# Token tiles taken chunk by chunk over the batches in a linear-attention and mixture-of-experts kernel

## The chip, the cores and the metric

The kernel runs on one core of one Trainium2 chip. The metric is the device time of one launch in microseconds (us), as the median of several runs. Engines are called PE (TensorE, with PEld for its weight loads), DVE (VectorE), ACT (ScalarE), POOL (GpSimd) and SP (SyncE, which here only issues DMAs).

## The reference, cut to what matters

```python
B, H, S, D = 4, 8, 768, 48              # q, k, v, alpha: [B, H, S, D], alpha in 0.8..1
for t in range(S):
    state = alpha[:, :, t, :, None] * state + k[:, :, t] (outer) v[:, :, t]   # [B, H, D, D]
    y[:, :, t] = q[:, :, t] @ state
x = y.transpose(0, 2, 1, 3).reshape(3072, 384)      # a row per token
do_compute = x @ w_skip > 0
e = argmax(x @ w_gate)                  # one of 8 experts, w1 384x1024, w2 1024x384
out = x                                 # for the tokens to skip
out = x + gate[e] * (relu(x @ w1[e]) @ w2[e])       # for the others
```

There are two halves: an attention whose state decays with every token, separately for each batch and head, and a layer in which each token goes to at most one of eight experts.

## The kernel before

**Attention.** A sequence of 768 tokens is cut into six chunks of 128. A token tile is one chunk of one batch, with all eight heads; there are 24. Heads go in four pairs: one head of a pair lies on partitions 0 to 47, the other on 64 to 111, and the tokens run along the free axis, one stretch per pair. For a tile the kernel does the following.

- `load` (L208) brings decays, q and k into one of five buffers (`qka`), and v (`vt`), four tiles ahead.
- `decay_suffix` (L224) runs a scan on DVE from the chunk's end to its start, which gives the products of the decays after a token (`sfx`); its last column is the decay of the whole chunk (`total`). POOL multiplies k by it. `decay_prefix` (L245) runs a second scan, forward, seeded with the reciprocal of the total (`pfx`); q is multiplied by it, on POOL, or on DVE for the first three tiles. Both are done three tiles ahead.
- `scores` (L253): eight products of k and q, one a head, into two PSUM buffers, one for each head of a pair. `causal` (L265) copies them under a mask to SBUF (`st`), a copy on DVE for each of the two.
- `turn_k` (L272) transposes k on PE, ACT copies it to SBUF (`kt`). `outer` (L293) makes from it and v what the chunk adds to the state (`ps_v`).
- `carry` (L324): state = (state + what the chunk adds) times the total of the next chunk, on DVE, in two instructions for each of the two heads' partitions. The states of a pair are one 112 x 112 block with zeros between the heads.
- `inter` (L282): output from the state, four products of 112 rows, one a pair. `intra` (L305): output from the chunk's own tokens, added in the same PSUM buffer `ps_y`, of which there are two; ACT copies the result to SBUF (`xt`).
- `rows` (L344): PE turns the output into rows of x and their logits (`ps_g`), DVE sums the logits, ACT copies the rows, SP stores them to the output. This runs one tile later.
- `guard` (L236): two passes on ACT over the tile's decays, each with a sum, which find decays outside 0.75 to 1.25. If one is there, a general path computes everything again at the end.

**Routing** works on groups of three tiles, from tile 18 on on single ones. A dozen small DVE instructions find the expert, the counts and the gate (`route_expert` L366, `route_one` L391); PE ranks the tokens within their expert (`route_rank` L411), and DVE makes slots of it (`route_slot` L422). POOL scatters the rows by slot to DRAM (`scatter` L483). `tick` (L361) emits the next of these small instructions between large ones. Weights of the first expert are loaded and split into two float32r parts meanwhile (`weight_pieces` L497, `split_pieces` L509).

**Order.** The order is written out by hand in `static_path` (L748); each engine runs its instructions in it. The 24 tiles go batch by batch, so tile i + 1 needs the state that tile i leaves, except at a batch's start. SP's queue holds a tile's loads, the clearing of the experts' slots (iterations 0 to 3, from a tile that POOL fills), pieces of weights, and the store of the rows of the tile before.

**Experts.** For each of the eight: rows are gathered, transposed and split in two (`turn` L548), four times a group of 18 products gives 256 columns of the hidden layer (`up` L563, three PSUM buffers, ACT and DVE split the result), 48 products give the output (`down` L584), and POOL scatters it. The next expert's weights are split, and those of the one after it loaded, in between. `must_redo` (L605) gathers the flag for the general path, in the third expert.

Of the kernel before, what the change touches and what calls it, by code (L numbers as in the profile page):

```python
# [44 lines left out]
GT = 3                  # token tiles that are routed at a time  # L45
SOLO = 18               # from this tile on, one at a time
A_MIN, A_MAX = 0.75, 1.25   # decays for which products over a chunk stay far inside float32's range
WARM0, WARMB = 12, 2      # products that keep the tensor engine's clock up where it waits for data
LATE = NT - 3           # from this tile on, rows for the first expert do not pass through DRAM
DECAY_MIN = 1e-18       # below A_MIN ** 128: keeps the reciprocal finite where the general path takes over  # L50
EG = 8                  # value columns that the general path scans at a time


class Kernel:
# [6 lines left out]
    # ---------------------------------------------------------------- constants  # L61
    def first_constants(self):
        """What the first chunk needs, and zeros for the clock warm-up."""
# [7 lines left out]
        # mask[s, (h t)]: 1 where s <= t  # L71
# [5 lines left out]
        self.mask = const.tile([P, 4 * P], U8, name="mask")  # L77
        self.mask_f = mask_f

        # sums of what the decays lie outside the range  # L80
# [243 lines left out]
    def carry(self, i):  # L324
        """The state after chunk i, scaled by the whole decay of chunk i + 1."""
        nc, w = self.nc, self.work[i]
        if i % C == C - 1:
            return
# [624 lines left out]
```

## Time and profile before

| what | value |
|---|---|
| time, median of 3 runs | 340.71 us (339.92 to 341.02) |
| span of the profiled execution | 338.5 us, 7103 instructions |
| between the span and the median | 2.2 us |
| mean granted clock of PE | 0.905 |
| attention, up to the experts' first product | 190.2 us |
| experts, to the end | 148.3 us |
| PE busy | 287.1 us (85%) |
| DVE busy | 246.8 us (73%) |
| ACT busy | 155.2 us (46%) |
| POOL busy | 181.2 us (54%) |

The profile is that of one execution. An engine's busy time is the sum over its instructions, overlaps counted once. A row of a group gives line, engine and operation, `out<-in`, shapes, the count, the busy time, the mean of one in ns, and behind the last bar the idle time of the engine just before it and who ended that. A row of the waits reads: engine and line that waited, `<-` whom it waited for: us in total, times, the longest. A row of the order of instructions gives start and duration in us. The granted clock is a share of full speed. The DMA share is the mean share of time in which the core's 16 DMA engines had a packet under way.

### The profile page before, as it was taken

Reading aid. Unit: us, or ns where it says so; the run is one execution under the profiler, and the core shown is the slowest. Engines: PE = TensorE matmul, PEld = TensorE weight load, DVE = VectorE, ACT = ScalarE, POOL = GpSimd, SP = SyncE. Lnnn points to the kernel's source line nnn. Section 1 sums busy time; section 2 is a strip of 40 time slices with the busy share of each in tenths; the row PEclk is TensorE's granted clock in tenths of the full one; section 3 lists DMA queues with packets and bytes.
Section 4 is the critical chain, followed back from the end, with each engine's and each line's share of the span. In section 5 each row is a group of like instructions: output and inputs, shape, how many; then the busy total and the mean of one; then the engine's idle time right before and its main releaser. Section 6 shows DMA issues by size and latency. Waiting matters only on the chain.

```text
span 338.5 us, 7103 instructions
## 1 busy us (share of the span) xinstructions
PE 287.1 (85%) x2618; PEld 273.1 (81%) x2618; DVE 246.8 (73%) x511; ACT 155.2 (46%) x344; POOL 181.2 (54%) x207
## 2 busy tenths in 40 slices
PE   5978859596696776859688899999999999999990
PEld 5867748495695766758587899999999999999990
DVE  8999997979979799999986583737465556455310
ACT  6336336543345462442355492827273736455200
POOL 7333454766686856874563445455454546464311
PEclk9579989878789597796969999999999999999998
DMA  8999999989666574794334473948475665751000
GB/s 237 285 228 254 251 249 221 262 212 225 152 141 146 137 175 79 160 247 136 113 118 157 153 239 126 300 157 260 187 242 212 212 235 191 270 175 58 8 26 20
DMA packets 27243, 61.42 MB, mean 181 GB/s; under 512 B 4338, under 2 KB 15328, under 8 KB 27200
## 3 DMA queue, kind: packets, MB, share of 16 engines
q1 hardware_dynamic: 24640, 56.04, 60.4%
q0 software_dynamic: 2560, 4.83, 4.1%
q8 instruction: 23, 0.38, 0.5%
q14 instruction: 20, 0.16, 0.2%
HBM read 48.15 MB, written 15.77 MB: 189 GB/s over the span
## 4 chain that ended last, share of the span: by engine, by line
PE 54%; DVE 34%; issue 4%; DMA 3%; POOL 3%; SPq 0%; POOLq 0%; ACT 0%; DVEq 0%
PE ps_h L577 20%; PE ps_o L593 20%; DVE pfx L249 6%; DVE sfx L228 6%; DVE st L269 5%; DVE state L340 4%; PE ps_g L352 4%; PE ps_y L290 4%; DVE tmp L337 3%; POOL cnt L386 2%; DMA qka<-in_qka_dram 2%; DVE eq L380 2%; PE ps_x L557 1%; PE ps_k L277 1%; DVE d L378 1%
## 5 line engine op out<-in xcount | busy, mean ns | idle before, releaser
L581 ACT ACTIVATE hh<-ps_h 128x512 fp32r<-128x512 f32 x32 | 19.2, 599 | 63.9 <-PE ps_h L577 63.9
L598 POOL DMA_INDIRECT out_dram<-o,xr x16 | 18.6, 1162 | 47.7 <-DVE o L596 44.4
L582 DVE SCALAR_TENSOR_TENSOR hl<-ps_h,hh 128x512 fp32r<-128x512 f32 x32 | 22.1, 691 | 30.1 <-ACT hh L581 30.1
L593 PE MATMUL ps_o<-w2h,hh 128*128 128x384 f32 x128 | 43.6, 341 | 0.0
L593 PE MATMUL ps_o<-w2h,hl 128*128 128x384 f32 x128 | 43.0, 336 | 0.0
L593 PE MATMUL ps_o<-w2l,hh 128*128 128x384 f32 x128 | 43.0, 336 | 0.0
L251 POOL TENSOR_TENSOR qka<-qka,pfx 112x512 f32<-112x512 f32 x21 | 26.5, 1263 | 29.3 <-DVE pfx L249 19.6
L234 POOL TENSOR_TENSOR qka<-qka,sfx 112x512 f32<-112x512 f32 x24 | 28.9, 1206 | 21.9 <-DVE sfx L228 19.4
L526 POOL TENSOR_TENSOR w2l<-raw,w2h 128x512 fp32r<-128x512 f32 x24 | 31.2, 1299 | 17.2 <-ACT w2h L522 16.8
L290 PE MATMUL ps_y<-qka,state 112*112 112x128 f32 x160 | 27.3, 322 | 13.0 <-DVE state L340 13.0
L488 POOL DMA_INDIRECT xs<-x,slot x24 | 31.4, 1309 | 10.2 <-DVE logit L353 3.1
L249 DVE TENSOR_TENSOR_SCAN pfx<-qka,seedb 112x516 f32<-112x516 f32 x24 | 35.7, 1489 | 0.5
L290 PEld LDWEIGHTS ps_y<-qka,state 112*112 112x112 f32 x160 | 22.4, 206 | 15.6 <-DVE state L340 11.7
L242 ACT ACTIVATE over<-qka,lim 112x512 bf16<-112x512 f32 x48 | 34.3, 719 | 0.1
L596 DVE SCALAR_TENSOR_TENSOR o<-ps_o,xr 128x384 f32<-128x384 f32 x16 | 9.9, 618 | 33.1 <-PE ps_o L593 33.1
L577 PE MATMUL ps_h<-xh,w1h 128*128 128x256 f32 x192 | 33.9, 282 | 0.0
L577 PE MATMUL ps_h<-xh,w1l 128*128 128x256 f32 x192 | 33.8, 282 | 0.0
L577 PE MATMUL ps_h<-xl,w1h 128*128 128x256 f32 x192 | 33.2, 282 | 0.0
L269 DVE COPY_PREDICATED st<-mask,ps_s 128x512 f32<-128x512 uint8 x46 | 31.8, 726 | 1.5 <-PE ps_s L261 0.9
L352 PE MATMUL ps_g<-xw,xt 112*128 112x105 f32 x184 | 32.8, 336 | 0.0
L352 PEld LDWEIGHTS ps_g<-xw,xt 112*128 112x128 f32 x184 | 30.6, 252 | 2.5 <-ACT ex L404 2.5
L261 PE MATMUL ps_s<-qka 48*128 48x128 f32 x368 | 28.7, 295 | 2.8 <-DVE qka L251 2.8
(148 smaller groups left out, 672.4 us busy)
## 6 DMA issues: line engine op xcount, KB each, us to landing
raw<-in_w_dram SPq DMA_DIRECT2D x64, 384.0 KB, 4.6
qka<-in_qka_dram SPq DMA_DIRECT2D x38, 288.9 KB, 5.3
vt<-in_v_dram SPq DMA_DIRECT2D x24, 192.0 KB, 6.8
out_dram<-x SPq DMA_DIRECT2D x24, 192.0 KB, 2.1
xr<-xs SPq DMA_DIRECT2D x18, 193.0 KB, 5.2
xs<-empty SPq DMA_DIRECT2D x8, 386.0 KB, 8.3
qka<-in_first_dram SPq DMA_DIRECT2D x3, 674.2 KB, 8.3
qka<-in_first_dram SPq DMA_DIRECT2D x2, 448.0 KB, 4.8
```

Of the source, the lines that this page charges most:

```text
L234: nc.gpsimd.tensor_tensor(w["kh"][:PD], w["kh"][:PD], seg(2)[:, :, 0:P], ALU.mult)
L242: nc.scalar.activation(out=over[:PD], in_=a, func=AF.Relu, scale=scale, bias=self.lim[:PD, j:j + 1], accum_out=self.odd[:PD, j, i:i + 1])
L249: nc.vector.tensor_tensor_scan(pfx[:PD].rearrange("p a t -> p (a t)"), w["qka"][:PD, 0:NP * SEG], w["seed"][:PD].rearrange("p a t -> p (a ...
L251: (eng or nc.gpsimd).tensor_tensor(w["qh"][:PD], w["qh"][:PD], pfx[:PD, :, 1:SEG], ALU.mult)
L261: nc.tensor.matmul(ps[h][:, p * P:(p + 1) * P], lhsT=kh[r, p, :], rhs=qh[r, p, :], start=True, stop=True)
L269: nc.vector.copy_predicated(w["st"][h], self.mask, w["ps"][h])
L290: nc.tensor.matmul(w["y"][:PD, p, :], lhsT=state[:PD, p, :], rhs=w["qh"][:PD, p, :], start=(p == 0), stop=False)
L352: nc.tensor.matmul(pg[:, p, :], lhsT=w["xt"][:PD, p, :], rhs=self.xw[:PD, p, :], start=True, stop=True)
L488: ins = nc.gpsimd.indirect_dma_start(out=self.xs[:, :], out_offset=bass.IndirectOffsetOnAxis(ap=self.slot[:, i, :], axis=0), in_=x, in_off ...
L526: eng.tensor_tensor(lo[:, s], raw[:, s], hi[:, s].bitcast(F32), ALU.subtract)
L577: nc.tensor.matmul(ps[:, u, :], lhsT=a[:, k, f * P:(f + 1) * P], rhs=b[:, k, :], start=(n == 0), stop=(n == len(order) - 1))
L593: nc.tensor.matmul(ps, lhsT=a[:, f, js], rhs=b[:, f, :], start=(n == 0), stop=(n == 3 * FT - 1))
```

## The change

1. **Order of tiles.** Tile i is chunk i // 4 of batch i % 4, so the four batches take turns and a state is needed four tiles later. There are four state buffers, one a batch. The host lays out the inputs in this order.
2. **Decays.** One function, `decay`, does both scans behind each other: first the forward one from the raw decays (`pfx`), then the reciprocal of the total, then the backward one seeded with it (`sfx`), so that k is divided by the product up to its token. Then POOL multiplies k and q (DVE does both for tiles 0 and 1). It stands at the start of an iteration.
3. **States** are compact, [112, 4 x 48]: sum and product with the total take one instruction each for both heads, and the total is the chunk's own. `inter` makes eight products of 48 rows, one a head, into two PSUM buffers, one for each head of a pair; each has one copy only, and ACT copies each to SBUF.
4. **Masked copy.** The scores of a tile lie in one PSUM buffer of two banks, of which there is one; one instruction copies all under a mask twice as wide.
5. **The check** of the decays leaves the attention. In the experts' stage alpha is loaded again in eight pieces of 128 x 1152 into one buffer, a piece after each half of an output, and ACT passes over each twice. `must_redo` moves from the third to the sixth expert.
6. Scores and transposed k are issued before the ranks; the splits and ticks stand at other places.

```diff
-NT = B * C              # token tiles
+NT = B * C
...
+GP = 8
+GW = B * H * S * D // P // GP
...
-        self.ps_s = st.enter_context(tc.tile_pool(name="ps_s", bufs=2, space=PSUM))
-        self.ps_y = st.enter_context(tc.tile_pool(name="ps_y", bufs=2, space=PSUM))
+        self.ps_s = st.enter_context(tc.tile_pool(name="ps_s", bufs=1, space=PSUM))
+        self.ps_y = [st.enter_context(tc.tile_pool(name=f"ps_y{h}", bufs=1, space=PSUM)) for h in range(2)]
...
-        self.state = [fix.tile([P, NP, PD], F32, name=f"state{i}") for i in range(2)]
+        self.state = [fix.tile([P, NP, D], F32, name=f"state{b}") for b in range(B)]
...
+    def decay(self, i, eng=None):
         nc, w = self.nc, self.work[i]
+        n = NP * SEG
+        pfx = self.sc.tile([P, NP, SEG], F32, name="pfx", bufs=5)
+        nc.vector.tensor_tensor_scan(pfx[:PD].rearrange("p a t -> p (a t)"), w["qka"][:PD, 0:n], self.seed1[:PD], 0.0,
+                                     ALU.mult, ALU.max)
+        w["total"] = pfx[:, :, P:SEG]
         seed = self.seedb[i % 2]
+        self.tick()
+        nc.vector.reciprocal(seed[:PD, SEG:AW:SEG], w["total"][:PD].rearrange("p a o -> p (a o)"))
+        self.tick()
+        sfx = self.sc.tile([P, n], F32, name="sfx")
+        nc.vector.tensor_tensor_scan(sfx[:PD, 0:n - 1][:, ::-1], w["qka"][:PD, 2:AW][:, ::-1], seed[:PD, 2:AW][:, ::-1],
+                                     0.0, ALU.mult, ALU.add)
+        after = sfx[:PD].rearrange("p (a s) -> p a s", s=SEG)[:, :, 0:P]
+        (eng or nc.gpsimd).tensor_tensor(w["kh"][:PD], w["kh"][:PD], after, ALU.mult)
         (eng or nc.gpsimd).tensor_tensor(w["qh"][:PD], w["qh"][:PD], pfx[:PD, :, 1:SEG], ALU.mult)
...
     def causal(self, i):
-        for h in range(2):
-            nc.vector.copy_predicated(w["st"][h], self.mask, w["ps"][h])
-            self.tick()
+        self.nc.vector.copy_predicated(w["st"], self.mask, w["ps"])
...
     def inter(self, i):
+        w["y"] = [pool.tile([P, NP, P], F32, name="ps_y") for pool in self.ps_y]
+        state = self.state[i % B]
+        if i // B > 0:
             for p in range(NP):
-                nc.tensor.matmul(w["y"][:PD, p, :], lhsT=state[:PD, p, :], rhs=w["qh"][:PD, p, :],
-                                 start=(p == 0), stop=False)
+                for h in range(2):
+                    r = slice(64 * h, 64 * h + D)
+                    nc.tensor.matmul(w["y"][h][r, p, :], lhsT=state[r, p, :], rhs=w["qh"][r, p, :],
+                                     start=(p == 0), stop=False)
...
     def carry(self, i):
+        if i // B == C - 1:
+            return
+        state = self.state[i % B]
+        src = w["pv"][:PD]
+        if i >= B:
+            tmp = self.sm.tile([P, NP, D], F32, name="tmp")
+            nc.vector.tensor_tensor(tmp[:PD], src, state[:PD], ALU.add)
             self.tick()
+            src = tmp[:PD]
+        nc.vector.tensor_tensor(state[:PD], src, w["total"][:PD].to_broadcast([PD, NP, D]), ALU.mult)
+        self.tick()
...
+    def guard(self):
+        nc = self.nc
+        part = B * NP // GP
+        for g in range(GP):
+            a = self.mp.tile([P, part, GW // part], F32, name="alpha", bufs=1)
+            src = self.nat[g * part:(g + 1) * part, 0].rearrange("o r t -> o (r t)").rearrange("o (p n) -> p o n", p=P)
+            nc.sync.dma_start(out=a, in_=src)
+            yield
+            for j, scale in enumerate((-1.0, 1.0)):
+                over = self.mp.tile([P, part, GW // part], BF16, name="over", bufs=1)
+                nc.scalar.activation(out=over, in_=a, func=AF.Relu, scale=scale, bias=self.lim[:, j:j + 1],
+                                     accum_out=self.odd[:, j, g:g + 1])
...
             for i in range(2):
-                self.decay_suffix(i)
-                self.decay_prefix(i, self.nc.vector)
+                self.decay(i, self.nc.vector)
             self.scores(0)
...
-            self.decay_suffix(2)
-            self.decay_prefix(2, self.nc.vector)
+            self.decay(2)
             clear = self.clear_pieces()
             for i in range(NT):
...
-                if i < NT - 1:
-                    self.guard(i)
-                advance(split, 1)
-                if i + 1 < NT:
-                    self.scores(i + 1)
+                if i + 3 < NT:
+                    self.decay(i + 3)
+                    self.tick()
...
+                if i + 1 < NT:
+                    self.scores(i + 1)
+                    self.turn_k(i + 1)
                 if ranked and not late:
                     self.route_rank(ranked)
                     self.small = chain(self.small, self.route_slot(ranked))
                 if i + 1 < NT:
                     self.causal(i + 1)
+                    self.tick()
+                advance(split, 1)
                 self.inter(i)
-                if i + 3 < NT:
-                    self.decay_suffix(i + 3)
-                    self.tick()
-                if i + 1 < NT:
-                    self.turn_k(i + 1)
...
-                if i + 3 < NT:
-                    self.decay_prefix(i + 3)
-                    self.tick()
                 if i < NT - 1:
                     self.intra(i)
...
                 for j in range(NB):
                     self.down(e, j)
                     advance(split, 2)
+                    advance(check, 1)
                 advance(fetch, 4)
```

More of the change, by code (lines that the diff above doesn't have):

```diff
@@ L229, in decay_suffix @@
                                      ALU.mult, ALU.max)
-        seg = lambda o: sfx[:PD, o:o + NP * SEG].rearrange("p (a s) -> p a s", s=SEG)
+        w["total"] = pfx[:, :, P:SEG]
         seed = self.seedb[i % 2]
-        w.update(total=seg(0)[:, :, 1:2], seed=seed)
-        nc.vector.reciprocal(seed[:PD, :, 0:1], w["total"])
-        nc.gpsimd.tensor_tensor(w["kh"][:PD], w["kh"][:PD], seg(2)[:, :, 0:P], ALU.mult)
-    def guard(self, i):
-        nc, t = self.nc, self.work[i]["qka"]
-        a = t[:PD, 0:NP * SEG].rearrange("p (a s) -> p a s", s=SEG)[:, :, 1:]
-        for j, scale in enumerate((-1.0, 1.0)):
-            over = self.sm.tile([P, NP, P], BF16, name="over")
-            nc.scalar.activation(out=over[:PD], in_=a, func=AF.Relu, scale=scale, bias=self.lim[:PD, j:j + 1],
-                                 accum_out=self.odd[:PD, j, i:i + 1])
@@ L245, in decay_prefix @@
-    def decay_prefix(self, i, eng=None):
-        nc, w = self.nc, self.work[i]
-        pfx = self.sc.tile([P, NP, SEG], F32, name="pfx")
-        nc.vector.tensor_tensor_scan(pfx[:PD].rearrange("p a t -> p (a t)"), w["qka"][:PD, 0:NP * SEG],
-                                     w["seed"][:PD].rearrange("p a t -> p (a t)"), 0.0, ALU.mult, ALU.add)
+        self.tick()
+        nc.vector.reciprocal(seed[:PD, SEG:AW:SEG], w["total"][:PD].rearrange("p a o -> p (a o)"))
+        self.tick()
+        sfx = self.sc.tile([P, n], F32, name="sfx")
@@ L255, in scores @@
         kh, qh = w["kh"], w["qh"]
-        pools = (self.ps_g, "ps_g"), (self.ps_n, "ps_n")
-        ps = [pool.tile([P, NP * P], F32, name=name) for pool, name in (pools if i == 1 else [(self.ps_s, "ps_s")] * 2)]
+        ps = self.ps_s.tile([P, 2, NP * P], F32, name="ps_s")
         for p in range(NP):
@@ L285, in inter @@
         nc, w = self.nc, self.work[i]
[L286 to L288 removed]
+        w["y"] = [pool.tile([P, NP, P], F32, name="ps_y") for pool in self.ps_y]
+        state = self.state[i % B]
+        if i // B > 0:
             for p in range(NP):
[L290 to L291 removed]
+                for h in range(2):
+                    r = slice(64 * h, 64 * h + D)
+                    nc.tensor.matmul(w["y"][h][r, p, :], lhsT=state[r, p, :], rhs=w["qh"][r, p, :],
+                                     start=(p == 0), stop=False)
     def outer(self, i):
         nc, w = self.nc, self.work[i]
[L296 removed]
+        if i // B < C - 1:
             w["pv"] = self.ps_v.tile([P, NP, D], F32, name="ps_v")
@@ L307, in intra @@
         nc, w = self.nc, self.work[i]
-        c = i % C
         ps, v = w["y"], w["v"]
@@ L312, in intra @@
                 o = (2 * p + h) * D
-                nc.tensor.matmul(ps[64 * h:64 * h + D, p, :], lhsT=v[:, o:o + D],
-                                 rhs=w["st"][h][:, p * P:(p + 1) * P], start=(c == 0 and p == 0), stop=(p == NP - 1))
+                nc.tensor.matmul(ps[h][64 * h:64 * h + D, p, :], lhsT=v[:, o:o + D],
+                                 rhs=w["st"][:, h, p * P:(p + 1) * P], start=(i < B and p == 0), stop=(p == NP - 1))
         xt = self.xtb[i % 2]
-        if c > 0:
-            nc.scalar.copy(out=xt[:PD], in_=ps[:PD])
-        else:
-            for h in range(2):
-                r = slice(64 * h, 64 * h + D)
-                nc.scalar.copy(out=xt[r], in_=ps[r])
+        for h in range(2):
+            r = slice(64 * h, 64 * h + D)
+            nc.scalar.copy(out=xt[r], in_=ps[h][r])
         w["xt"] = xt
@@ L858, in static_path @@
             self.late_split(b)
-            self.x0t = [pool.tile([P, CAP], F32, name=name) for pool, name in
-                        ((self.ps_s, "ps_s"), (self.ps_s, "ps_s"), (self.ps_g, "ps_g"))]
+            ps = self.ps_s.tile([P, 2, NP * P], F32, name="ps_s")
+            self.x0t = [ps[:, 0, :CAP], ps[:, 1, :CAP], self.ps_g.tile([P, CAP], F32, name="ps_g")]
             self.route_rank((a, b))
@@ L890, in static_path @@
                 fetch = self.weight_pieces(e + 2) if e + 2 < E else iter(())
+                if e == 0:
+                    check = self.guard()
                 if e + 2 < E:
```

70 lines of the change are left out of this document (25 added, 45 removed).

## The prediction

> **What bounds the kernel now.** I read the page's head first, then the busy time by stretch, the groups by line, the chain of waits, and last the order of instructions in single tiles.
>
> ```profile
> span 338.5 us, 7103 instructions
> 0.00:190.00 190.00, 146.31 (x1614) 132.74 (x1615) 171.86 (x392) 86.97 (x213) 114.68 (x155) 0.84 0.77 190
> 15.00:70.00 55.00, 43.09 (x520) 39.02 (x520) 51.38 (x103) 25.72 (x61) 27.38 (x36) 0.87 1.02 245
> 70.00:190.00 120.00, 92.14 (x1030) 83.49 (x1030) 107.13 (x270) 53.70 (x136) 79.11 (x100) 0.83 0.64 156
> 190.00:331.00 141.00, 140.84 (x1006) 140.35 (x1004) 74.49 (x120) 68.28 (x131) 65.56 (x52) 1.00 0.52 178
> 190.19 8.62 PE ps_h L577 x72
> ```
>
> The columns of a stretch are its length, then PE, PEld, DVE, ACT and POOL busy, the granted clock, the DMA share and GB/s. The last row is a piece of the chain: there the experts begin. From then on PE is busy for 140.84 of 141 us at clock 1.00. Before it, in the attention, VectorE is the fullest engine, 171.86 of 190 us, while PE has 146.31 us at a mean clock of 0.84. The attention falls into two: from 15 to 70 us the DMA engines are full as well (share 1.02), from 70 us on they are not (0.64). The median of the runs, 340.71 us, is 2.2 us above the span; I add that to every span.
>
> The pace is read from the stores of finished rows, one a tile (start and duration of the issue):
>
> ```profile
> 25.83 0.36 SPq L359 DMA_DIRECT2D out_dram<-x  x1
> 71.88 0.34 SPq L359 DMA_DIRECT2D out_dram<-x  x1
> 178.92 0.34 SPq L359 DMA_DIRECT2D out_dram<-x  x1
> ```
>
> They are those of tiles 0, 7 and 21: 6.6 us a tile at first, 7.6 us later (107.04 over 14)..
>
> **The change, part by part.** What VectorE does, mean of one instruction behind the bar:
>
> ```profile
> L249 DVE TENSOR_TENSOR_SCAN pfx<-qka,seedb 112x516 f32<-112x516 f32 x24 | 35.7, 1489 | 0.5
> L228 DVE TENSOR_TENSOR_SCAN sfx<-qka,seed 112x517 f32<-112x517 f32 x24 | 30.3, 1262 | 0.5 <-DMA qka<-in_qka_dram 0.3 <-DMA qka<-in_first_dram 0.2
> L269 DVE COPY_PREDICATED st<-mask,ps_s 128x512 f32<-128x512 uint8 x46 | 31.8, 726 | 1.5 <-PE ps_s L261 0.9
> L340 DVE TENSOR_TENSOR state<-tmp,sfx 48x192 f32<-48x192 f32 x32 | 16.7, 522 | 0.9
> L340 DVE TENSOR_TENSOR state<-ps_v,sfx 48x192 f32<-48x192 f32 x8 | 2.8, 349 | 0.1
> L337 DVE TENSOR_TENSOR tmp<-ps_v,state 48x192 f32<-48x192 f32 x32 | 11.2, 351 | 2.7 <-PE ps_v L302 2.4
> L353 DVE TENSOR_REDUCE logit<-ps_g 128x9 f32<-128x36 f32 x23 | 4.2, 183 | 6.5 <-PE ps_g L352 6.4
> L251 DVE TENSOR_TENSOR qka<-qka,pfx 112x512 f32<-112x512 f32 x3 | 2.9, 957 | 0.1
> L192 DVE CAST mask<-mask_f 128x512 uint8<-128x512 f32 x1 | 0.6, 637 | 0.0
> 101.85 1.19 POOL L234 TENSOR_TENSOR qka<-qka,sfx 112x512 f32<-112x512 f32 x1
> 101.93 2.20 DVE L249 TENSOR_TENSOR_SCAN pfx<-qka,seedb 112x516 f32<-112x516 f32 x1
> 110.79 1.22 DVE L249 TENSOR_TENSOR_SCAN pfx<-qka,seedb 112x516 f32<-112x516 f32 x1
> ```
>
> *Masked copy.* Two copies of 512 elements cost 1.45 us a tile. One of 1024: an operation of 36 elements takes 0.18 us, so 0.55 us of the 0.726 goes by size, and the merged one takes 0.18 + 2 x 0.55 = 1.28 us. Saving 0.17 us.
>
> *Compact states.* The sum and the product ran once a head on 48 rows, 192 elements each; now once a tile on 112 rows. Both run along the free axis, so I keep the time of one: 2 x 0.351 + 2 x 0.522 = 1.75 us become 0.35 + 0.35 = 0.70 us. The 0.35 for the product is the undisturbed row; at the disturbed mean of 0.522 it is 0.17 us worse. Saving 1.05 us.
>
> *Scans.* Both remain, with almost the same length. But a scan of 1.22 us took 2.20 us where GpSimd's product of k started beside it. Before, k's product starts after the first scan and meets the second on its way; now both products start behind the second scan, and the masked copy follows on VectorE. So 1.489 + 1.262 become 2 x 1.22 at best: a saving of 0 to 0.31, of which I take 0.25.
>
> That is 1.45 us a tile. Not all is kept, since the two products now stand in a row on GpSimd:
>
> ```profile
> L234 POOL TENSOR_TENSOR qka<-qka,sfx 112x512 f32<-112x512 f32 x24 | 28.9, 1206 | 21.9 <-DVE sfx L228 19.4 <-PE ps_y L313 2.0 <-issue 0.4
> L251 POOL TENSOR_TENSOR qka<-qka,pfx 112x512 f32<-112x512 f32 x21 | 26.5, 1263 | 29.3 <-DVE pfx L249 19.6 <-DVE on L400 2.9 <-DVE slot L437 2.3
> ```
>
> They hold 2.5 us after the scan. Behind it VectorE has the masked copy (1.28), the logits (0.18), the sum (0.35) and small routing steps: some 2.2 us, then the state's product, which reads two buffers in SBUF as the scan does. Routing steps and weight splits that do the same can be caught earlier. Bounds: nothing, to a whole product, 1.2 us a tile; I take 0.35, near the lower end, because the order fits. Net gain 1.1 us a tile: 7.6 becomes 6.5.
>
> The Trainium skill, "SBUF — State Buffer", section "Who interferes with whom", says that a VectorE instruction with two SBUF inputs contends with a GpSimd instruction that reads SBUF, and that the loser blocks in full. By that rule alone, with 2.5 us of products against 2.2 us of other work, the loss would be 0.3 us a tile at most and the sum 1 us lower; the 2.20 us row agrees with it.
>
> *Where this gain counts.* Up to 70 us the DMA engines are full. The change moves the same bytes in the attention, so I credit nothing for tiles 0 to 7. For the 16 others: 16 x 1.1 = 17.6 us.
>
> *PE.* One tile at full clock, from its rows:
>
> ```profile
> 101.96 1.13 PE L290 MATMUL ps_y<-qka,state 112*112 112x128 f32 x8
> 102.93 0.55 PE L277 MATMUL ps_k<-ident,qka 112*128 112x112 f32 x4
> 103.31 1.05 PE L352 MATMUL ps_g<-xw,xt 112*128 112x105 f32 x8
> 104.29 0.56 PE L302 MATMUL ps_v<-vt,kt 128*48 128x48 f32 x16
> 104.69 1.05 PE L313 MATMUL ps_y<-st,vt 128*48 128x128 f32 x16
> 96.87 1.16 PE L261 MATMUL ps_s<-qka 48*128 48x128 f32 x16
> 114.68 1.90 PE L352 MATMUL ps_g<-xw,xt 112*128 112x105 f32 x8
> ```
>
> Together 5.5 us (a float32 product is two instructions). The product with the state goes from four of 112 rows to eight of 48. The scores, also eight of 48 rows, take 1.16 us, as long as four wide ones (1.13): the heads of a pair run side by side. So I add nothing; without that overlap it is 1.1 us, still near VectorE's 6.5. What goes is the wait on the state: it now comes from four tiles back.
>
> ```profile
> PE ps_y L290 <- DVE state L340: 13.0, 9, 2.8
> PE ps_n L418 <- POOL cnt L386: 19.5, 5, 4.5
> ```
>
> PE is not the end there, so I count only what returns through VectorE's waits for the logits (6.4 us in the row above). Scores and transposed k are now issued before the ranks, so that wait shrinks: -2 us. Single score and output buffers cost nothing while PE is ahead: the next scores wait for a masked copy that ends some 4 us into VectorE's tile. ScalarE gets a second copy of the outputs, some 0.6 us as for other copies of 512 elements; the check, which leaves it, took 2 x (0.719 + 0.193) us.
>
> *Start.* Tiles 0 and 1 now have k's product on VectorE too, tile 2 has q's on GpSimd: one more at 0.96, and a mask twice as large, 0.637. The slots' clearing waits for GpSimd, now behind both products of tile 2, and the loads of tile 5 are queued behind it on SP. With the DMA full this is lost: bounds 0 and 4 us, I take +2.
>
> *The check.* ScalarE has half its time free in the attention: no gain there. Its place in the experts:
>
> ```profile
> L242 ACT ACTIVATE over<-qka,lim 112x512 bf16<-112x512 f32 x48 | 34.3, 719 | 0.1
> L242 ACT ACTIVATION_READ_ACCUMULATOR over<-qka,lim 112x1 f32 x48 | 9.3, 193 | 0.0
> L581 ACT ACTIVATE hh<-ps_h 128x512 fp32r<-128x512 f32 x32 | 19.2, 599 | 63.9 <-PE ps_h L577 63.9
> L357 ACT COPY x<-ps_g 128x384 f32<-128x384 f32 x23 | 11.0, 480 | 34.9 <-DVE logit L353 17.9 <-issue 7.2 <-POOL x L356 4.5
> L522 ACT CAST w2h<-raw 128x512 fp32r<-128x512 f32 x48 | 27.0, 628 | 0.0
> L582 DVE SCALAR_TENSOR_TENSOR hl<-ps_h,hh 128x512 fp32r<-128x512 f32 x32 | 22.1, 691 | 30.1 <-ACT hh L581 30.1
> ACT hh L581 <- PE ps_h L577: 63.9, 31, 6.7
> raw<-in_w_dram SPq DMA_DIRECT2D x64, 384.0 KB, 4.6
> ```
>
> Eight loads of 576 KB go into one buffer: each waits on SP for the check before it, with four weight loads behind it. A pair of passes over 1152 elements takes between 1.8 us (no growth) and 4.1 us (all by size). ScalarE's copies of 384 and 512 elements, 0.480 and 0.599, grow by 0.93 ns an element; with 640 more a pass I take 2 x (0.719 + 0.193 + 0.6) = 3.0. Experts 1 to 3 have two pairs, 6.0 us, with one landing between them, 4.6 us by the weight row, at worst 6.9 by size, less 1.25 for two weight casts. That is 9.35 to 11.65 us against 6.7 idle, so ScalarE comes 2.65 to 4.95 us late to the next expert. PE has three buffers and fills one in 8.62 / 4 = 2.16 us; it stalls when the first isn't free two fillings later, 4.3 us, of which 0.6 and 0.7 go to the two passes that empty it: 3.0 us of lateness are covered. So 0 to 1.95 us for each of three experts; I take +2 in all. Without the buffers it would be 8 to 15.
>
> **Sum:** -17.6 - 2 + 2 + 2 = -15.6, from 340.7: **325 us**.
>
> **Rivals.** *More gain:* the DMA share of 1.02 isn't a limit, the tiles before 70 us gain too (8 x 1.1) and half of VectorE's 18 us of idle goes: 325 - 9 - 9 = 307 to 316. For: VectorE idles only 0.5 us before the first scan. Against: a full share for 55 us.
>
> *PE becomes the bound:* it starts every tile waiting for the one score buffer and the clock stays at the 0.84 of now: 5.5 / 0.84 = 6.6 us a tile, and at the slow row (1.90 for 1.05) much more; with 0.4 us over my 6.5 it gives 331. Against: a PE that is the bound isn't idle.
>
> The Trainium skill, "TensorE: Matmul & The Clock Gate", section "A second HAM failure mode: psum-queue depth-cycling", tells of small idle gaps between groups that make the clock swing; no row here shows gaps under 1 us doing so.
>
> *Loads late:* tile loads, issued after the rows' store, land too late for the earlier scan in all tiles; half the gain is left, 333.
>
> *Slower:* the check's chain in the experts. If ScalarE's full lateness reaches PE and the weights behind the alpha loads come late too, 4.9 us for each of four experts are lost, 20 us; it decides from 4.4 us on. 340.7 - 17.6 + 20 = 343. Against: the three buffers.
>
> *Not what it says:* products per head don't pair and all is given back: 340.
>
> **Numbers.** Forecast (318 to 330) 0.52, more gain 0.15, PE 0.14, loads 0.09, slower 0.07, no change 0.03. Under 0.3% either way, 1 us, a measurement can't tell from no change. Faster 0.90, same 0.03, slower 0.07. The range leaves out half of "more gain" and the slower end: 312 to 336.
>
> **What would show it.** The experts' first product comes at 172 to 177 us; state and sum together 36 instructions near 0.35 us; the masked copy near 1.28; the scans' means below 1.3; the stores 6.3 to 6.7 us apart after tile 8, and about 6.6 before; PE over 138 us busy in the experts' 143. Wrong: scans still near 1.49, a PE clock below 0.8 with PE full, or gaps in PE in experts 1 to 3.

## The result, and the profile after

The changed kernel takes 333.0 us (median of 4 runs, 329.7 to 333.9) against 340.9 of the kernel before on the same chip: ratio 0.974, interval 0.968 to 0.979. The forecast was 325 us with a range of 312 to 336. The ratio goes by the fast runs alone, those within 1.5% of a kernel's fastest, and is not the quotient of the medians, which are over all runs. Sign and range hold, but the inner forecast of 318 to 330 us was missed; the gain, 7.9 us by the medians and 9.0 by the ratio, is about half of what was forecast.

The profiled execution took 333.5 us, its span is 331.8 us, 6.7 less than before. To see where these came from I cut both attentions at the stores of rows of tiles 0, 7, 17, 18 and 22 and at the experts' first product. This is the busy time by stretch, first of the kernel before, then of the changed one (length, PE, PEld, DVE, ACT and POOL busy, granted clock, DMA share, GB/s):

```profile
25.83:71.88 46.05, 36.17 (x452) 32.84 (x450) 41.35 (x90) 21.97 (x53) 24.59 (x34) 0.90 1.03 244
71.88:147.57 75.69, 58.14 (x668) 52.66 (x665) 69.84 (x139) 34.59 (x83) 54.18 (x64) 0.84 0.70 157
147.57:158.16 10.59, 7.34 (x71) 6.70 (x70) 10.11 (x24) 3.70 (x10) 7.04 (x10) 0.68 0.70 199
158.16:184.40 26.24, 20.75 (x244) 18.57 (x241) 22.20 (x83) 11.19 (x32) 12.67 (x19) 0.87 0.42 128
184.40:190.03 5.63, 4.06 (x38) 3.89 (x36) 4.70 (x25) 3.75 (x12) 3.46 (x5) 1.00 0.62 189
190.03:338.50 148.47, 140.81 (x1006) 140.32 (x1004) 74.95 (x120) 68.28 (x131) 66.50 (x53) 0.99 0.50 170
```

```profile
25.45:73.56 48.11, 42.95 (x531) 37.32 (x529) 35.95 (x75) 16.40 (x33) 22.80 (x34) 0.84 1.01 252
73.56:140.15 66.59, 56.22 (x772) 48.27 (x770) 63.03 (x116) 26.75 (x54) 57.66 (x65) 0.95 0.79 186
140.15:150.72 10.57, 5.95 (x87) 4.79 (x83) 10.02 (x25) 1.76 (x5) 7.06 (x12) 0.99 0.64 166
150.72:176.50 25.78, 22.96 (x210) 18.45 (x211) 14.80 (x65) 9.20 (x23) 11.28 (x17) 0.74 0.45 136
176.50:182.31 5.81, 4.46 (x42) 4.19 (x40) 4.48 (x25) 2.37 (x8) 3.60 (x5) 1.00 0.68 217
182.31:331.80 149.49, 141.42 (x1005) 140.53 (x1004) 75.49 (x120) 88.28 (x163) 67.18 (x53) 0.99 0.56 198
```

Read them in pairs. Tiles 7 to 17 gained 9.1 us (0.91 a tile), with VectorE 92% busy before and 95% after. Of the 9.1 us, 6.8 are VectorE's work (69.84, 63.03) and 2.3 its idle time: its waits for the logits in this stretch went from 3.8 to 1.3 us. From the store of tile 17 to the experts nothing came: 42.46 us before, 42.16 after. From tile 17 to 18 VectorE is full on both sides and its work did not fall (10.11, 10.02). In the fourth row it fell from 22.20 to 14.80 us; yet the stretch kept its length (26.24, 25.78), and now PE is the fullest engine, 22.96 us, at a clock of 0.74. The first store came 0.4 us earlier and tiles 0 to 7 took 2.1 us longer (46.05, 48.11), though VectorE had 5.4 us less to do there, so tile 7 is 1.7 us late; the experts lost 1.0. The experts' first product, forecast for 172 to 177 us, came at 182.3.

The groups that the forecast priced came out so:

```profile
L233 DVE TENSOR_TENSOR_SCAN pfx<-qka,seed 112x516 f32<-112x516 f32 x24 | 34.0, 1418 | 11.0 <-DMA qka<-in_qka_dram 11.0
L241 DVE TENSOR_TENSOR_SCAN sfx<-qka,seedb 112x515 f32<-112x515 f32 x24 | 32.3, 1347 | 1.5
L261 DVE COPY_PREDICATED st<-mask,ps_s 128x1024 f32<-128x1024 uint8 x24 | 30.9, 1286 | 0.0
L325 DVE TENSOR_TENSOR state<-tmp,pfx 112x192 f32<-112x192 f32 x16 | 8.9, 554 | 0.2
L322 DVE TENSOR_TENSOR tmp<-ps_v,state 112x192 f32<-112x192 f32 x16 | 5.6, 348 | 1.4 <-PE ps_v L295 1.4
```

The masked copy is at the 1.28 us forecast, the sum at 0.35, the product with the state at 0.55 instead of 0.35; the scans kept 1.38 on average, not 1.22. At full clock the product with the state takes 1.08 us for 16 instructions (the row at 129.06 below): the heads do run side by side.

Here is the place after tile 17, from the order of instructions of the changed kernel:

```profile
129.06 1.08 PE L283 MATMUL ps_y<-qka,state 48*48 48x128 f32 x16
...
142.76 0.97 POOL L474 DMA_INDIRECT xs<-x,slot  x1 [0.28 <-issue]
143.19 2.95 DVE L233 TENSOR_TENSOR_SCAN pfx<-qka,seed 112x516 f32<-112x516 f32 x1
143.76 1.28 POOL L512 TENSOR_TENSOR w2l<-raw,w2h 128x512 fp32r<-128x512 f32 x1
147.54 1.27 DVE L261 COPY_PREDICATED st<-mask,ps_s 128x1024 f32<-128x1024 uint8 x1
148.91 1.16 PE L254 MATMUL ps_s<-qka 48*128 48x128 f32 x16 [3.65 <-POOL qka L244]
151.22 2.54 PE L283 MATMUL ps_y<-qka,state 48*48 48x128 f32 x16 [1.15 <-ACT xt L310]
153.79 2.02 PE L337 MATMUL ps_g<-xw,xt 112*128 112x105 f32 x8
```

A scan takes 2.95 us beside GpSimd's scatter and weight split, so the masked copy behind it ends at 148.81. The next scores need the one score buffer that this copy empties (the row names GpSimd's product of k, which ends beside it at 148.88; but at 33.13 us the scores began while that product ran on to 33.15, and there as here they began 0.10 us behind the masked copy's end): PE idles 3.65 us, then 1.15 us more for ScalarE's output copies, and from then on its rows double, 2.54 us for the 1.08 above and 2.02 for the 1.12 that the rows of a tile take at full clock. Theories after this reading: **A**, the single output buffers and ScalarE's second copy starve PE in the late tiles; **B**, VectorE's order does, with the masked copy behind both scans; **C**, the chain of routing steps sets these tiles whatever the rest does. The clock came in as a fourth on the way.

### The profile page after: what moved, and what is told of

Same layout as the page of the kernel before. It is cut to its first block, busy times and chain, and to the rows that moved or that the text cites. A ratio compares the mean times of both kernels' runs of the same rounds, so it can differ in the third digit from the quotient of the medians.

```text
span 331.8 us, 7365 instructions
## 1 busy us (share of the span) xinstructions
PE 292.5 (88%) x2778; PEld 270.2 (81%) x2778; DVE 226.9 (68%) x453; ACT 152.6 (46%) x298; POOL 184.3 (56%) x205
## 5 line engine op out<-in xcount | busy, mean ns | idle before, releaser
L254 PE MATMUL ps_s<-qka 48*128 48x128 f32 x384 | 31.8, 308 | 23.8 <-POOL qka L244 12.0
L254 PEld LDWEIGHTS ps_s<-qka 48*128 48x128 f32 x384 | 26.9, 209 | 29.0 <-POOL qka L244 13.5
L582 DVE SCALAR_TENSOR_TENSOR hl<-ps_h,hh 128x512 fp32r<-128x512 f32 x32 | 22.1, 690 | 33.5 <-ACT hh L581 33.3
L593 PE MATMUL ps_o<-w2h,hh 128*128 128x384 f32 x128 | 43.6, 341 | 0.0
L233 DVE TENSOR_TENSOR_SCAN pfx<-qka,seed 112x516 f32<-112x516 f32 x24 | 34.0, 1418 | 11.0 <-DMA qka<-in_qka_dram 11.0
L343 ACT COPY x<-ps_g 128x384 f32<-128x384 f32 x23 | 11.0, 480 | 65.5 <-DVE logit L338 23.7
L512 POOL TENSOR_TENSOR w2l<-raw,w2h 128x512 fp32r<-128x512 f32 x24 | 31.2, 1302 | 13.5 <-ACT w2h L508 13.1
L474 POOL DMA_INDIRECT xs<-x,slot x24 | 29.9, 1244 | 12.2 <-DVE on L386 4.9
L310 ACT COPY xt<-ps_y 48x512 f32<-48x512 f32 x48 | 27.8, 580 | 13.6 <-PE ps_y L305 12.8
L241 DVE TENSOR_TENSOR_SCAN sfx<-qka,seedb 112x515 f32<-112x515 f32 x24 | 32.3, 1347 | 1.5
L305 PE MATMUL ps_y<-st,vt 128*48 128x128 f32 x384 | 32.9, 313 | 0.0
L512 POOL TENSOR_TENSOR w1l<-raw,w1h 128x512 fp32r<-128x512 f32 x16 | 22.3, 1395 | 18.7 <-issue 10.4
L581 ACT ACTIVATE hh<-ps_h 128x512 fp32r<-128x512 f32 x32 | 19.1, 597 | 27.6 <-PE ps_h L577 27.6
L261 DVE COPY_PREDICATED st<-mask,ps_s 128x1024 f32<-128x1024 uint8 x24 | 30.9, 1286 | 0.0
```

Source lines behind the costliest of these rows:

```text
L233: nc.vector.tensor_tensor_scan(pfx[:PD].rearrange("p a t -> p (a t)"), w["qka"][:PD, 0:n], self.seed1[:PD], 0.0, ALU.mult, ALU.max)
L241: nc.vector.tensor_tensor_scan(sfx[:PD, 0:n - 1][:, ::-1], w["qka"][:PD, 2:AW][:, ::-1], seed[:PD, 2:AW][:, ::-1], 0.0, ALU.mult, ALU.add)
L254: nc.tensor.matmul(ps[:, h, p * P:(p + 1) * P], lhsT=kh[r, p, :], rhs=qh[r, p, :], start=True, stop=True)
L261: self.nc.vector.copy_predicated(w["st"], self.mask, w["ps"])
L305: nc.tensor.matmul(ps[h][64 * h:64 * h + D, p, :], lhsT=v[:, o:o + D], rhs=w["st"][:, h, p * P:(p + 1) * P], start=(i < B and p == 0), sto ...
L310: nc.scalar.copy(out=xt[r], in_=ps[h][r])
```

## The experiments

All ratios are to the kernel before in the same series. "Half" is the time at half clock between the stores of tiles 18 and 22: in rows of half a us the clock is 1.0 or 0.5 but where it changes, so it is 2 x (1 - clock) x length of the stretch. The clock is read to two digits, so this is good to some 0.3 us.

| kernel | median us | ratio (interval) | tiles 7-17 | 17-18 | 18-22 | half |
|---|---|---|---|---|---|---|
| before | 340.9 | 1 | 75.7 | 10.6 | 26.2 | 6.8 |
| changed | 333.0 | 0.974 (0.968-0.979) | 66.6 | 10.6 | 25.8 | 13.4 |
| two output tiles | 332.3 | 0.976 (0.971-0.980) | 66.7 | 10.6 | 22.8 | 6.8 |
| one output copy | 331.4 | 0.973 (0.969-0.977) | 67.5 | 10.4 | 22.1 | 5.7 |
| copy first | 341.7 | 0.993 (0.989-0.997) | 71.6 | 10.7 | 27.1 | 13.5 |
| clear early | 329.9 | 0.965 (0.962-0.969) | 67.4 | 10.6 | 25.2 | 16.6 |
| states per head | 342.6 | 1.006 (1.001-1.012) | 73.0 | 11.4 | 24.1 | 7.2 |
| order of before | 332.6 | 0.976 (0.972-0.980) | 66.5 | 9.1 | 25.4 | 11.7 |
| check back | 329.8 | 0.967 (0.963-0.970) | 67.3 | 10.6 | 22.3 | 6.7 |
| zeros, tile 16 | 335.4 | 0.976 (0.969-0.984) | 67.9 | 10.6 | 23.2 | 7.0 |
| zeros, tiles 16 to 19 | 332.3 | 0.971 (0.965-0.978) | 67.6 | 10.6 | 24.4 | 13.7 |
| three edits | 327.0 | 0.960 (0.955-0.966) | 66.7 | 10.5 | 23.2 | 15.3 |
| three edits, zeros | 326.0 | 0.956 (0.951-0.962) | 67.4 | 10.6 | 18.0 | 0 |
| the same, split earlier | 327.5 | 0.960 (0.956-0.963) | 71.5 | 9.0 | 21.7 | 0 |

The stages are those of one profiled execution each. Executions of one kernel lie one to three per cent apart, so differences are told by the ratios, and a stage's few us in one profile are a hint, not a proof.

**Two output tiles, and one output copy.**

```
-  self.ps_y = [... tile_pool(name=f"ps_y{h}", bufs=1, space=PSUM) for h in range(2)]
+  self.ps_y = ... tile_pool(name="ps_y", bufs=2, space=PSUM)
-  w["y"] = [pool.tile([P, NP, P], F32, name="ps_y") for pool in self.ps_y]
+  w["y"] = [self.ps_y.tile([P, NP, P], F32, name="ps_y")] * 2
```

> Both heads of a tile go into one output tile, and there are two of these again, as in the kernel before; still one ScalarE copy a head. Theory A (the last six tiles are bound by PE and ScalarE: the product with the state waits for both copies of the tile before, 8.2 us in the trace after, and PE falls to half clock in the gaps): the waits of ps_y for ScalarE are gone, from tile 17 to the experts' first product 42.2 us become 39 to 40, and the time falls by 2 to 4 us. Theory B (the masked copy's place on VectorE behind both scans starves PE): the waits go, but the stage stays within 1 us of 42.2 and the time within 1 us. Theory C (the chain of routing steps a tile sets the pace, whatever the buffers): no change either.

The second kernel adds, with the state's first head 64 columns wide:

```
+  if i >= B:
+      nc.scalar.copy(out=xt[:PD], in_=ps[0][:PD])
+  else: ...
```

> As the run with two output tiles, and from the second chunk on one ScalarE copy of 112 rows for both heads instead of two of 48, the state's first head padded with zeros to 64 columns so that all 112 rows are written. Theory A: it gains 0.6 us more in each tile whose chain goes through ScalarE, so 1 to 3 us beyond the run with two tiles, most of it after tile 17, since the Exp of the routing on which VectorE waits ahead of the masked copy (1.12 us at 165.67) is queued behind these copies. Theories B and C: within 1 us of the changed kernel.

In the profiles tiles 18 to 22 took 3.0 and 3.7 us less, as A has it; 17 to 18 didn't move, and from tile 17 to the experts it took 39.6 us in both. PE's waits of 2.8 us for the output copies are gone. But the ratios, 0.976 and 0.973, are that of the changed kernel, and the second kernel's further 1 to 3 us did not come. Two later kernels that leave the output buffers as they are (check back, and zeros behind tile 16) took 39.0 and 39.6 us from tile 17 to the experts as well. So A's waits are real and their price isn't settled by these two. What the profiles also differ in is the clock:

```profile
150.93:173.03 22.10, 19.59 (x221) 16.58 (x217) 17.32 (x78) 7.89 (x25) 14.23 (x20) 0.87 0.48 141
```

This is the kernel with one copy from the store of tile 18 to that of 22: 0.87 where the changed kernel had 0.74.

**Masked copy ahead of the scans.**

```
+  self.causal(i + 1)
+  self.tick()
   self.decay(i + 3)
   self.tick()
   ...
-  self.causal(i + 1)
-  self.tick()
```

> In every tile the masked copy of the next tile goes ahead of the two scans of the tile three on, instead of behind them; nothing else. Theory B: PE's idle time before the scores (23.8 us after the change) falls to under 10 us; the gap of 10.6 us between the stores of tiles 17 and 18 becomes 7 to 8; the time falls by 3 to 6 us. Theory A: it gains at most 1 us, since the waits for the output copies stay. A rival against it: the masked copy now waits for PE on VectorE itself, and the scans and GpSimd's products come later; then it is slower, by up to 0.5 us a tile, 8 us.

The rival was right, by the ratios 6.6 us slower than the changed kernel. PE's idle time before the scores fell from 23.8 to 5.0 us, as B had it, but its waits for the output copies grew from 2.8 to 11.8, and B's gain did not come: the step from 17 to 18 stayed at 10.7. The groups of this kernel say why:

```profile
L261 DVE COPY_PREDICATED st<-mask,ps_s 128x1024 f32<-128x1024 uint8 x24 | 31.0, 1294 | 6.0 <-PE ps_s L254 6.0
L325 DVE TENSOR_TENSOR state<-tmp,pfx 112x192 f32<-112x192 f32 x16 | 13.2, 822 | 0.4
L369 DVE SCALAR_TENSOR_TENSOR m<-logit,eq 128x24 bf16<-128x24 f32 x6 | 4.9, 809 | 0.0
```

VectorE now waits 6.0 us for the scores itself. And behind the scans, when GpSimd runs its two products, there is no longer the masked copy, which takes 1.29 us either way, but the state's product and the routing: 0.82 us for 0.55, and 0.81 for 0.17 (170 ns in the changed kernel). The place of the copy in the change is part of the gain.

**Clear early.**

```
+  self.make_empty()        # memset and iota of the zero row, moved out of clear_pieces
   self.decay(2)
   clear = self.clear_pieces()
```

> The zero row for clearing the slots is made on GpSimd ahead of the two products of tile 2, not behind them; nothing else. The first clear is issued near 16 us instead of 20.4, the load of tile 5 near 17.5 instead of 22.9. The forecast's term (the late start is lost because the DMA engines are full): the store of tile 4 comes about 2 us earlier, at 53 to 54 us instead of 55.8, and the experts' first product 2 us earlier, the time -2. Rival (VectorE's later gaps swallow it, or the loads were not late by this): the store of tile 8 and the time within 0.7 us of the changed kernel.

```profile
11.42 0.93 SPq L152 DMA_DIRECT2D xs<-empty  x2
```

The first clear is issued at 11.42 instead of 20.44, the load of tile 5 at 14.26 instead of 22.92, and the store of tile 4 comes at 53.03 instead of 55.80 (52.36 before the change). By the ratios it is 2.8 us faster; the two intervals overlap by a little. In the four kernels with this edit that store lies at 53.0 to 54.1, in the eight others made from the change at 53.6 to 58.1. The forecast's +2 for the start fits these numbers, though the two ranges overlap.

**States once a head again.**

```
-  nc.vector.tensor_tensor(tmp[:PD], src, state[:PD], ALU.add)
-  nc.vector.tensor_tensor(state[:PD], src, w["total"][:PD]..., ALU.mult)
+  for h in range(2):
+      r = slice(64 * h, 64 * h + D)
+      ...
+      nc.vector.tensor_tensor(tmp[r], src, state[r], ALU.add)
+      nc.vector.tensor_tensor(state[r], src, w["total"][r]..., ALU.mult)
```

> The changed kernel with the state's sum and product once a head again (48 rows, 192 elements) instead of once a tile on 112 rows: two instructions of about 0.35 us more in each of 16 tiles, one more in four. If VectorE sets the pace of tiles 7 to 17 (the forecast's ground), that stage takes 0.7 us a tile more, 73 to 75 us instead of 66.6, and the time is 7 to 12 us longer, 340 to 345. If the gain came from elsewhere (the waits on the state and the ranks that went), the stage stays under 69 us and the time within 3 us of the changed kernel.

```profile
76.08:149.10 73.02, 62.91 (x765) 54.14 (x763) 70.18 (x137) 26.81 (x53) 43.29 (x64) 0.84 0.71 163
```

Tiles 7 to 17 take 73.0 us, 0.64 a tile more; VectorE is busy 70.18 of them. By the ratios the time is 11 us above the changed kernel's, and slightly above that of before. So undoing the compact states alone takes back the whole gain of the change. With VectorE's work as before the change (70.18, 69.84 us) the stage is still 2.7 us shorter (73.02, 75.69): that part of the 9.1 us is less idle time of VectorE, not less work.

**Order of before.** All six chunks of a batch in a row, by `i % C` and `i // C` in place of `i // B` and `i % B`, and the layouts to match.

> The changed kernel with the tiles in the order of before, all six chunks of a batch in a row, so that a tile's product with the state needs the state made in the tile just before; the rest of the change stays. Forecast's theory (the wait on the state is off the path, VectorE is the end): PE waits again for the state, about 10 us in all, but the stage of tiles 7 to 17 keeps 64 to 68 us and the time is within 2 us of the changed kernel. Rival (the order is what earns the gain): 5 to 8 us slower.

```profile
76.03:142.57 66.54, 56.42 (x701) 48.34 (x698) 64.60 (x112) 25.83 (x52) 57.47 (x65) 0.87 0.80 182
```

332.6 us, tiles 7 to 17 in 66.54: the order alone is worth nothing here, as the forecast had it. But PE's wait on the state did not come back, 0.6 us where 10 were expected, so the run doesn't show what such a wait would cost. And the equal time is a sum: the store of tile 7 came 2.5 us later than in the changed kernel, the step from 17 to 18 took 1.5 less.

**Check back in the attention.**

```
+  if i < NT - 1:
+      self.guard(i)          # two passes of Relu over the tile's decays, as before
   ...
-  advance(check, 1)
```

> The changed kernel with the check of the decays on ScalarE in the attention again, two passes a tile, and no loads for it in the experts. Theory (forecast: the check costs 2 us in the experts, its removal from the attention brings nothing): from the experts' first product to the end 148.0 to 148.5 us instead of 149.5, the first product where it was, so 1 to 2 us faster. Rival (ScalarE is on the path in the late tiles, where Exp stands behind its copies, so the passes cost there): the experts gain the same, but from tile 17 to the first product it takes 2 to 5 us more than 42.2.

```profile
178.54:326.30 147.76, 140.93 (x1005) 140.44 (x1004) 75.19 (x120) 68.13 (x131) 66.40 (x53) 0.98 0.49 169
```

The experts take 147.76 us, 1.7 less than after the change; in the three later kernels with this edit it is 147.8 each, in all others made from the change 148.8 to 151.3. The late tiles were no slower (39.0 us from tile 17 to the experts, 42.2 after the change), so the rival falls. By the ratios the kernel gains 2.4 us, with intervals that overlap. Moving the check made no stage clearly faster: tiles 7 to 17 took 67.3 us with it back, and between 66.5 and 67.9 in most kernels made from the change.

**Zeros on TensorE behind tile 16.**

```
+  if i in (16,):
+      self.hold(12)          # 12 products of zeros into ps_k
```

> Twelve products of zeros on TensorE behind tile 16's last product, where it idled 3.65 us (145.26 to 148.91) and then ran at a granted clock of 0.59 for the next 8 us; nothing else. Clock theory (PE at half clock is the end of the late tiles): the stretch of 8 us behind the gap keeps a clock above 0.9, the product with the state after it takes 1.1 instead of 2.5 us, and from tile 17 to the experts' first product it takes 38 to 40 us instead of 42.2; the time falls by 2 to 4 us. Rival (VectorE and the routing set these tiles, the half clock only fills idle time): the clock is held, the stage stays within 1 us of 42.2.

I had counted the tiles wrong: the gap of 3.65 us lies behind tile 19's last product. The products ran at 126.19, 2.94 us for their 24 instructions, and the gap stayed (3.66 us), as did the half clock behind it. As a test of the clock it tells nothing. Yet from tile 17 to the experts this profile took 39.6 us, inside the 38 to 40 of the clock theory; it is of a run of 330.7 us, the other runs took 335.2 to 338.3. A stage of one profile can lie 2.6 us off without the cause that was to be tested.

**Zeros behind tiles 16 to 19.** Ten profiles lay side by side by then, and the column "half" was made.

> The earlier twelve zero products stood behind tile 16, but the gap of 3.65 us lies behind tile 19's last product; now thirteen stand there (3.2 us at the 0.123 us of one instruction that the earlier run showed) and four behind each of tiles 16 to 18; nothing else. In ten profiles the stretch from the store of tile 18 to that of tile 22 took 22.1 to 23.2 us where PE had 5.6 to 6.9 us of half clock in it and 25.2 to 27.1 where it had 11.8 to 16.4 (with VectorE's own work as after the change). Clock theory: with the gap filled, no more than 7 us of half clock, the stretch takes 20 to 23 us, and the median of the runs falls by 2 to 3 us against the changed kernel's 333.0. Rival (the half clock comes for another reason than the gap, or these products use up what the clock allows): half-clock time and median as before, or up to 2 us slower.

```profile
151.17:175.58 24.41, 22.69 (x210) 18.98 (x211) 14.85 (x65) 9.08 (x23) 11.26 (x17) 0.72 0.47 139
```

The gap was filled but for 0.56 us, and still the clock fell: a wait of 1.14 us for ScalarE's output copies followed (theory A's), then 13.7 us of half clock. The ratio is that of the changed kernel. Filling the one long gap isn't enough. The runs of this kernel follow the clock granted over the whole span (328.3 us at 0.947, 332.8 at 0.927); those of the kernel with two output tiles do not (330.8 at 0.906, 334.5 at 0.926).

**Three edits together**: check back, clear early, one output copy; and **the three with the zeros**.

> Three of the edits tried together: the check of the decays back on ScalarE in the attention, the zero row made ahead of tile 2's products, and both heads' outputs in one of two tiles with one ScalarE copy. If each costs in its own stage (check 1.7 us in the experts, clear 2 to 3 us in tiles 0 to 4, outputs up to 2.5 us in the late tiles when the clock allows): 333.0 - 1.7 - 2.5 - 1 = 327 to 329, from the store of tile 0 to that of tile 4 27 us, experts 147.8. If the gains take each other away (ScalarE's passes delay the output copies, VectorE catches up in the middle anyway): 330 to 331.

> The three edits and the zero products behind tiles 16 to 19. Clock theory: 1 to 3 us below the three edits alone, with 7 us of half clock or less from the store of tile 18 to that of tile 22. Rival: no difference beyond 1 us.

```profile
71.28:138.00 66.72, 60.44 (x756) 52.45 (x754) 63.71 (x115) 34.31 (x83) 57.70 (x65) 0.85 0.78 177
148.54:171.77 23.23, 22.96 (x216) 19.81 (x215) 15.07 (x66) 10.57 (x33) 12.18 (x17) 0.67 0.44 135
```

```profile
149.70:167.68 17.98, 15.25 (x206) 13.17 (x203) 14.38 (x65) 10.25 (x30) 12.16 (x17) 1.00 0.59 175
```

The first two lines are of the three edits, tiles 7 to 17 and 18 to 22, the last of the kernel with the zeros, 18 to 22. The gains add up within their intervals: 0.960, 327.0 us, 4.5 below the changed kernel by the ratios. With the zeros the profiled execution has no half clock after tile 17 at all, and tiles 18 to 22 take 18.0 us. PE's work in them is 15.25 us where half clock made it 22.96. This profile is of a run of 323.0 us, the median is 326.0. Between the two kernels the medians differ by 1.1 us, and their intervals overlap: what the zeros are worth over many runs is open.

**Weights split one tile earlier**, on top (`if i == 6` for `if i == 7`).

> The three edits and the zero products, with the first expert's weights split one tile earlier, so that GpSimd's last piece of it (1.29 us at 142.74 in the profile of the version before this one) no longer lies beside the scan that took 2.94 us there. Theory (from the store of tile 17 to that of tile 18 VectorE is full, and what GpSimd takes from it there is lost): that scan takes about 1.7 us, the stretch 9.2 to 9.4 us instead of 10.56, and the time is 1 to 1.5 us below the version before, if PE keeps its clock in the tiles after. Rival (something else is met instead, or the chain to the next store runs through other engines): the stretch stays at 10.2 to 10.6.

```profile
153.46:175.18 21.72, 19.41 (x242) 16.17 (x241) 16.40 (x77) 11.83 (x36) 13.63 (x20) 1.00 0.49 144
```

The scan took 1.23 us there and the step from 17 to 18 9.0 us: that GpSimd's work holds VectorE in this step is shown. The order of before, where the split met the other scan, has a step of 9.1 us too. But the time didn't fall. This profile is of a run of 331.0 us, the median is 327.5. Tiles 18 to 22 took 3.7 us more than in the version before, at full clock, with 36 more PE instructions and 4.2 us more of PE busy. Only five of the 36 are zero products, sixteen are scores: the masked copy ended at 151.56, but the scores began at 153.94, when the thirteen zero products (150.85 to 154.01) were done. So zeros sized for a gap that was no longer there cost some 2.3 us. Tiles 7 to 17 took 4 us more, with no more work on VectorE (63.75 us, 64.87 in the version before): it waited 6.4 us for PE instead of 1.6, with 20.5 us of half clock in the stretch instead of 6.8. Why the clock fell there is open.

## Why the prediction was right, and why it gave twice the gain

By its own steps, on the spans:

| step | forecast | measured |
|---|---|---|
| start, tiles 0 to 7 | +2 | +1.7 |
| tiles 7 to 17 | 10 of the 16 x 1.1: -11 | -9.1 |
| waits for the logits, no stage named | -2 | -2.5 in tiles 7 to 17, within their -9.1 |
| tile 17 to the experts | the other 6 x 1.1: -6.6 | -0.3 |
| check in the experts | +2 | +1.0 |
| sum | -15.6 | -6.7 |

**What VectorE saves.** The mechanism was right and the middle shows it: the middle shortens when VectorE gets less to do, and grows by 0.64 us a tile when the states are made twice again. The term of 1.1 us a tile came out as 0.91 of time, of which 0.68 is VectorE's work and the rest its shorter waits. By the means of the priced groups VectorE saves 1.0 us a tile. The masked copy was met exactly. Too small was the loss to GpSimd, 0.45 us a tile where 0.35 were taken: the two scans saved nothing of 0.25 us (1418 + 1347 ns against 1489 + 1262), and the state's product took 0.55 us for 0.35. The scans' means, forecast below 1.3 us, stayed above it. That nothing was credited up to tile 7 fits: there VectorE had 5.4 us less work and waited 10.7 us for loads.

**Where this gain counts.** This is the step that failed: "For the 16 others: 16 x 1.1". The last six tiles were credited with VectorE's gain as if VectorE set their pace. It gave up 7.4 us of work from tile 18 to 22, and PE took its place: with "Single score and output buffers cost nothing while PE is ahead" I had seen the buffers but not that PE isn't ahead in these tiles. There PE waits for the masked copy and the output copies, its clock halves, and then it is PE that is late. A PE clock below 0.8 with PE full was a sign of being wrong that the prediction named; here it is 0.74 with PE busy 89%. The chain of work that ended last says the same (start, duration, what):

```profile
167.27 1.23 DVE pfx L249
170.47 1.88 PE ps_g L352 x8
```

```profile
165.37 1.08 PE ps_y L283 x14
167.58 1.92 PE ps_y L305 x16
169.54 0.59 ACT xt L310
170.17 2.54 PE ps_y L283 x16
172.71 1.84 PE ps_y L305 x16
```

Before the change (the first two lines) it runs almost only through VectorE from 147 to 170.3 us. In the changed kernel it runs through PE and an output copy from 165.3 to 175.7; it can't be followed further back. The first of the six tiles is another case: from 17 to 18 VectorE stayed full, and the scan that lost 1.7 us to GpSimd ate the gain. Without that loss the step took 9.0 us in the last experiment.

The rival "PE becomes the bound" had this, at 331 us and a chance of 0.14, but for all tiles. In the middle it mostly fails: there 6.7 us of half clock (changed), 17.3 (order of before) and 20.0 (three edits) gave 66.6, 66.5 and 66.7 us, since VectorE is the end; only the last kernel took 71.5, with as much half clock as the three edits and VectorE waiting for PE.

From 18 to 22, with VectorE's work as after the change, the longer stretches tend to be those with more half clock. Of the kernels with single output tiles, two with 6.7 and 7.0 us of it took 22.3 and 23.2 us, five with 11.7 to 16.6 took 24.4 to 27.1; of those with two, 22.1 and 22.8 with 5.7 and 6.8, 23.2 with 15.3, and 18.0 with none. (The last kernel, 21.7 with none, lost 2.3 us to its zero products.) Over the whole stretch from tile 17 to the experts the order is looser: half clock took 13.7 us of it before and after the change alike, and kernels with that much needed 39.0 (check back) to 43.6 us (copy first). Only with 0 and 3.4 us of it did the stretch fall to 34.3 (three edits, zeros) and 37.1 (the same, split earlier). The 34.3 us are 8.1 less than before; but that kernel has three more edits besides the zeros, and it is one profile. That the missing gain went to the clock fits this, and is not shown. Theory C doesn't hold as stated: the routing was never touched, and this stretch took 34.3 to 43.6 us.

What makes the clock fall is less sure. Zeros in the long gap alone left 13.7 us of half clock; zeros with two output tiles left none. That the gaps are the cause is likely, and not shown.

The Trainium skill, "TensorE: Matmul & The Clock Gate", section "HAM oscillation — how this bites in real kernels", sets the rule at PE idling over some 3.4 us. The trace agrees for the gap of 3.65 us, but in the kernel with two output tiles a single gap of 1.46 us (138.04 to 139.50), after ten busy us, was followed by half clock within 1.5 us, and one of 1.93 us in the changed kernel (to 126.54) and one of 2.25 us in the kernel with three edits and zeros were not; so the measurement decides, and length alone does not. The other section that the prediction names, on small gaps between groups, fits better than I gave it credit for: with zeros behind tiles 16 to 19, gaps of 0.56 and 1.14 us (to 149.37 and 151.67) came ahead of the half clock from 153.2 on.

**Loads late**, 333 us in the forecast, gave the right time for the wrong reason: the waits of the scans for loads are 11.0 us, but 10.7 of them lie before 60 us, where nothing had been credited.

**Check and order.** Right in sign; the check's two passes take 2.7 us with their reads, where 3.0 were taken, and cost the experts 1.0 us against before and 1.7 by undoing them, within the bounds of 0 to 5.85. The waits of the changed kernel show where ScalarE's time went:

```profile
ACT hh L581 <- PE ps_h L577: 27.6, 16, 6.7
ACT over L545 <- DMA alpha<-in_nat_dram: 16.0, 4, 5.3
```

ScalarE waited 63.9 us for the experts' first products before; now it waits 27.6 for them and 16.0 for the check's loads. PE is still busy 141.42 of 149.49 us, so its idle time there grew by only 0.4 us (7.7, 8.1). The order of the tiles was rightly priced at nothing.

## What to carry to other kernels

A gain on the fullest engine counts tile by tile only as far as that engine sets the pace; cut the span into stages, find the engine that is full in each, and credit the gain there alone. Where the engine that comes next has a clock of its own, price its rows at the slower clock too. Undo the parts of a change one by one: here undoing the compact states took back the whole gain, and three smaller things around them cost 4.5 us. Look at several profiles before a stage's few us are put down to an edit.

## What the runs showed of the hardware

The half clock comes in pieces of 3.4, 6.8, 10.2, 13.7 or 17.1 us, most often 6.8: after the change one of 6.8 us at 89.0 us, with zeros behind tiles 16 to 19 one of 13.7 at 153.2, with the early clear one of 17.1 at 147.8. The Trainium skill, "TensorE: Matmul & The Clock Gate", section "Part 1: The HAM clock gate", speaks of a free-running window of about 3.4 us; the pieces are one to five of these.

An instruction of VectorE with two inputs in SBUF can lose more than one GpSimd instruction's time: the scan of 1.23 us took 2.95 beside a scatter (0.97 us) and a weight split (1.28 us) that followed each other.
